# Retention in one fixed order of TensorE, the combine softmax taken once, and the zeros in longer rows

## The chip, the cores and the metric

The kernel runs on one core of a Trainium2 chip. The metric is the time of one launch on the device in microseconds (us), the median of three runs. A core has TensorE (PE, with its weight loads as PEld), VectorE (DVE), ScalarE (ACT), GpSimd (POOL) and SyncE (SP). Each works through its own list of instructions in order. SP issues most of the DMA transfers here, which 16 DMA engines carry out.

## The reference

Retention over q, k, v (4 batches, 8 heads, 768 tokens, 64 wide) gives x of 3072 tokens by 512. A soft mixture of experts with 32 slots follows, and after it a noisy top-2 mixture with 8 experts of width 1024.

```python
for t in range(S):                                   # retention
    state = gamma * state + einsum('bhd,bhe->bhde', k[:, :, t], v[:, :, t])
    y[:, :, t] = scale * einsum('bhd,bhde->bhe', q[:, :, t], state)
logits = x @ phi                                     # soft mixture, phi: 512 x 32
d = softmax(logits, axis=0)                          # dispatch: over the 3072 tokens
slot_out[e] = relu((d.T @ x)[e] @ w1[e]) @ w2[e]     # 8 experts, 4 slots each
c = softmax(logits, axis=1)                          # combine: over the 32 slots
x2 = c @ slot_out
noisy = x2 @ w_gate + log1p(exp(x2 @ w_noise)) * noise   # top-2 mixture
out[mask] += top2_w * (relu(x2[mask] @ v1[e]) @ v2[e])
```

## The kernel before

All arithmetic of the retention is f32. The kernel has four stages one after the other.

**Retention.** The 3072 tokens are 24 chunks of 128, six to a batch. `comp` holds q and the spread k and v of even chunk pairs, `raws` the k and v as they land. A chunk j needs, on TensorE: `k_t` (four transposes of k into `pt`, L273, copied to `kT` by ACT), `q_t` (the same for q, L262, scaled to `qT` by two products on DVE), `qk` (L283, eight matmuls into `pa`; two DVE products with the mask make `am`, L287), `y_out` (the part from the state, L301, four matmuls of `sbd` by `qT`, left out at the first chunk of a batch; then L305, eight matmuls of v by `am`; DVE scales `py` to `xT`, L308), `kv` (L316, the state in `pS`; ACT copies its two halves to `sbd`, L321) and `x_n` (L326, `xT` turned back, copied by ACT to `x`). ACT spreads k into each chunk's layout (two copies, L246), POOL spreads and scales v (L247).

Every four chunks `todo` brings five pieces of the soft mixture: `group0` (L336, the logits `pl`, copied to `LT`; the running maximum on DVE; the exponential `dT` on ACT), `group1` (L362, `dT` turned), `group2` (L371, the dispatch product `pp`, added to `acc` by DVE), `group3` (L380, `LT` turned; the combine softmax over the slots in `cs` by DVE and ACT; two DMAs to `ctab`, L393) and `group4` (L398, `cs` turned into `cT`). The loop on j writes these pieces down in one order, but the scheduler of the framework sets the order of each engine by its own estimate of times, save where `after` ties an instruction behind another. TensorE's list therefore has pieces of one product between those of another.

SP's list carries q, k and v (512 KB each for a pair of chunks), 28 pieces of 512 KB of the first weights W1 (L456), and 24 DMAs that write zeros to `out` (L460, 256 KB each, in rows of 512 bytes, from a tile `zt` of 128 by 128 that DVE makes anew for each, in two buffers, L459). A piece of W1 is paced by a one-element copy on DVE that reads `xT` (L455).

**Slots.** After the last chunk the last group's pieces, the sum over the tokens and `psi` (L507); then the loop `ph` over eight experts (L516, W1) with the last `group3` after e = 2 and the last `group4` after e = 3; then the loop `po` over eight experts (L549, W2), with a filler of six matmuls on ones (L142) ahead of e = 7, and W2 loaded by SP as buffers come free.

**Routing** (the logits of the second mixture, the top two, the lists of tokens) and the **main mixture** stand after that, and the change doesn't touch their code; they read `cT`, `ctab` and `out`.

What sets the order of the loads, and the pace of the loop, stands in these lines:

```python
if g == 0 and t and t + 1 < NT:
    load_kv(t + 1)             # the DMAs and the copies of a pair, one call
...
for i in range(NCH * (j - 1) // ZP, NCH * j // ZP if j <= ZP else 0):   # ZP = 21
```

Of the kernel before, what the change touches and what calls it, by code (L numbers as in the profile page):

```python
# [21 lines left out]
P = 128  # L22
# [17 lines left out]
ZP = 21  # L40
# [4 lines left out]
RL = 1  # L45
FS, FU, FV = 10, 2, 2
# [57 lines left out]
def kernel(ctx: ExitStack, tc: tile.TileContext, q, k, v, phi, w1, w2,  # L104
# [61 lines left out]
    cT = ab.tile([P, NG, P], F32, name="cT")  # L166
# [37 lines left out]
    with ExitStack() as actx:  # L204
# [22 lines left out]
        def load_kv(u, gs=range(2)):  # L227
            b, t = divmod(u, NC // 2)
            raw = RAW.setdefault(u, [])
            for i, src in enumerate(() if raw else (k, v)):  # L230
                x = raws[:, 2 * (u % 2) + i]
                nc.sync.dma_start(x.rearrange("p h r d -> p h (r d)"),
                                  src[b, :, 256 * t:256 * t + 256, :].rearrange("h (p r) d -> p h (r d)", r=2))
                raw.append(x)
            for g in gs:
                j = 2 * u + g
                if u % 2:
                    KL[j] = io.tile([P, H, D], F32, name="kl", bufs=2)
                    VL[j] = io.tile([P, H, D], F32, name="vl", bufs=2)
                else:  # L240
                    KL[j], VL[j] = (comp[:, 2 + i].rearrange("p h r d -> p (h r d)")[:, DM * g:DM * g + DM]
                                    .rearrange("p (h d) -> p h d", h=H) for i in range(2))
                gs = slice(64 * g, 64 * g + 64)
                for r in range(2):
                    rs = slice(64 * r, 64 * r + 64)
                    nc.scalar.copy(KL[j][rs], raw[0][gs, :, r, :])  # L246
                    pool_ins[0] = nc.gpsimd.tensor_tensor(VL[j][rs], raw[1][gs, :, r, :],  # L247
                                            gv[gs, r, t, :, None].to_broadcast([64, H, D]), op=OP.mult)
# [8 lines left out]
        def q_t(t, s):  # L257
            if s == 0:
                QT[t] = io.tile([P, HP, 2, P], F32, name="qT", bufs=2)
            pt = psA.tile([P, HP, P], F32, name="pt", tag="pt")  # L260
            for hp in range(HP):
                nc.tensor.transpose(pt[:, hp, :], QL[t][:, 2 * hp + s, :, :], ident)  # L262
            o = QT[t].rearrange("p h g (r i) -> p h g r i", r=2)
            i = pt.rearrange("p h (g i) -> p h g i", g=2)
            for r in range(2):
                rs = slice(64 * r, 64 * r + 64)
                nc.vector.tensor_tensor(o[64 * s:64 * s + 64, :, :, r, :], i[rs],  # L267
                                        gq[rs, :, s, None, :].to_broadcast([64, HP, 2, 64]), op=OP.mult)

        def k_t(j):  # L270
            pt = psA.tile([P, HP, P], F32, name="pt", tag="pt")
            for hp in range(HP):
                nc.tensor.transpose(pt[:, hp, :], KL[j][:, 2 * hp:2 * hp + 2, :], ident)  # L273
            KT[j] = io.tile([P, HP, P], F32, name="kT", bufs=2)
            return nc.scalar.copy(KT[j], pt)  # L275
# [18 lines left out]
        def y_out(j):  # L294
            t, g = divmod(j, 2)
            c = j % NC
            py = psA.tile([P, HP, P], F32, name="py")
            am = [AM.pop((j, s)) for s in range(2)]
            if c:
                for hp in range(HP):  # L300
                    nc.tensor.matmul(py[:, hp, :], sbd[c % 2][:, hp, :], QT[t][:, hp, g, :],  # L301
                                     start=(hp == 0), stop=False, skip_group_check=True)
            for hp in range(HP):
                for s in range(2):
                    nc.tensor.matmul(py[64 * s:64 * s + 64, hp, :], VL[j][:, 2 * hp + s, :],  # L305
                                     am[s][:, hp, :], start=(not c and hp == 0), stop=True, skip_group_check=True)
            XT[j] = work.tile([P, HP, P], F32, name="xT", bufs=4)
            nc.vector.tensor_tensor(XT[j], py, gy[:, c, :, None].to_broadcast([P, HP, P]), op=OP.mult)  # L308

        def kv(j):  # L310
# [3 lines left out]
            for hp in range(HP):  # L314
                for s in range(2):
                    nc.tensor.matmul(pS[64 * s:64 * s + 64, hp, :], KL[j][:, 2 * hp + s, :],  # L316
                                     VL[j][:, 2 * hp + s, :], start=(c == 0 and hp == 0),
                                     stop=True, skip_group_check=True)
            for s in range(2):
                r = slice(64 * s, 64 * s + 64)  # L320
                nc.scalar.copy(sbd[(c + 1) % 2][r, :, r], pS[r])  # L321

        def x_n(j):
            pt = psA.tile([P, HP, P], F32, name="pt", tag="pt")
            for hp in range(HP):
                nc.tensor.transpose(pt[:, hp, :], XT[j][:, hp, :], ident)  # L326
            X[j] = work.tile([P, DM], F32, name="x", bufs=5)
            nc.scalar.copy(X[j], pt.rearrange("p h e -> p (h e)"))

        GR, NM = {}, []  # L330

        def group0(g):
            pl = psA.tile([P, P], F32, name="pl", tag="pg", bufs=1)
            for kd in range(KD):
                for i in range(4):
                    nc.tensor.matmul(pl[32 * i:32 * i + 32, :], phis[:, kd, :], XT[4 * g + i][:, kd, :],  # L336
                                     start=(kd == 0), stop=(kd == KD - 1), skip_group_check=True)
            LT = small.tile([P, P], F32, name="LT", bufs=1)
            nc.scalar.copy(LT, pl)
            m = MZ[:, g:g + 1]  # L340
            z = MZ[:, NG + g:NG + g + 1]
            nc.vector.reduce_max(m, LT, axis=AX.X)
# [11 lines left out]
            nc.scalar.activation(dT, LT, AF.Exp, bias=nm, accum_out=z)  # L354
            if g:
                nc.vector.scalar_tensor_tensor(z, z0, al, z, op0=OP.mult, op1=OP.add)
            GR[g] = [LT, dT, al]

        def group1(g):
            LT, dT, al = GR[g]  # L360
            pd = psA.tile([P, P], F32, name="pd", tag="pg", bufs=1)
            nc.tensor.transpose(pd, dT, ident)  # L362
            dn = small.tile([P, P], F32, name="dn", bufs=1)
            nc.scalar.copy(dn, pd)
            GR[g] = [LT, dn, al]

        def group2(g):
            _, dn, al = GR[g]
            pp = psA.tile([P, DM], F32, name="pp", tag="pt")
            for i in range(4):  # L370
                nc.tensor.matmul(pp[32 * i:32 * i + 32, :], dn[:, 32 * i:32 * i + 32], X[4 * g + i],  # L371
                                 start=True, stop=True, skip_group_check=True)
# [4 lines left out]

        def group3(g):
            pl = psA.tile([P, P], F32, name="pln", tag="pg", bufs=1)
            nc.tensor.transpose(pl, GR.pop(g)[0], ident)  # L380
            cs = small.tile([P, 4, NS], F32, name="cs", bufs=1)
            nc.scalar.copy(cs, pl.rearrange("p (i s) -> p i s", s=NS))
            mx = small.tile([P, 4], F32, name="mx")
            nc.vector.reduce_max(mx, cs, axis=AX.X)
            nc.vector.tensor_tensor(cs, cs, mx[:, :, None].to_broadcast([P, 4, NS]), op=OP.subtract)
            nc.scalar.activation(cs, cs, AF.Exp)
            sm = small.tile([P, 4], F32, name="sm")
            nc.vector.reduce_sum(sm, cs, axis=AX.X)
            nc.vector.tensor_scalar_add(sm, sm, 1e-9)
            nc.vector.reciprocal(sm, sm)  # L390
            nc.vector.tensor_tensor(cs, cs, sm[:, :, None].to_broadcast([P, 4, NS]), op=OP.mult)
            for r in range(2):
                nc.gpsimd.dma_start(row_view(r)[:, 4 * g:4 * g + 4, :NS], cs[64 * r:64 * r + 64])  # L393
            GR[g] = cs

        def group4(g):
            pc = psA.tile([P, P], F32, name="pc", tag="pg", bufs=1)
            nc.tensor.transpose(pc, GR.pop(g).rearrange("p i s -> p (i s)"), ident)  # L398
            nc.vector.tensor_copy(cT[:, g, :], pc)

        NT = NCH // 2
        ov = out.rearrange("(p a) d -> p a d", p=P)
# [3 lines left out]
        load_kv(0, range(1))  # L406
        nc.scalar.dma_start(phis, phi.rearrange("(k p) s -> p k s", p=P))
        for s in range(2):
            q_t(0, s)
        fill(psA, "py", FU)  # L410
        k_t(0)
        fill(psA, "py", FV)
        load_kv(0, range(1, 2))
        load_q(1)
        load_kv(1, ())
        qk0 = qk(0)
        with after(qk0):
            q_t(1, 0)
        todo = []
        for j in range(NCH + 1):  # L420
            t, g = divmod(j, 2)
            if g == 0 and t and t + 1 < NT:
                load_kv(t + 1)
            if j < NCH:
                if j + 1 < NCH:
                    kt = k_t(j + 1)
                    if j < 1:
                        with after(kt):
                            load_kv(1)
                    if todo:  # L430
                        todo.pop(0)()
                    qk(j + 1)
                tn, s = (t + 1, 1) if g == 0 else (t + 2, 0)
                if tn < NT:
                    q_t(tn, s)
                if todo:
                    todo.pop(0)()
                y_out(j)
                if g == 0 and t + 2 < NT:
                    load_q(t + 2)  # L440
                with after(*([qk0] if j == 0 else [])):
                    kv(j)
            if j:
                if j == NCH:
                    group0(NG - 1)
                x_n(j - 1)
# [4 lines left out]
                for i in range(28 * (j - 1) // WP, 28 * j // WP if j <= WP else 0):  # L451
                    if i % 4 == 0:
                        W1[i // 4] = (ringp if i < 8 else ringa).tile([P, 4096], F32, name="w", tag="w")
                    s = slice(1024 * (i % 4), 1024 * (i % 4) + 1024)
                    nc.vector.tensor_copy(W1[i // 4][0:1, s][:, 0:1], XT[j - 1][0:1, 0, 0:1])  # L455
                    nc.sync.dma_start(W1[i // 4][:, s], w1[i // 4].rearrange("(p k) n -> p (k n)", p=P)[:, s])  # L456
                for i in range(NCH * (j - 1) // ZP, NCH * j // ZP if j <= ZP else 0):
                    zt = small.tile([P, P], I32, name="zt")
                    nc.vector.tensor_single_scalar(zt, XT[j - 1][:, 0, :].bitcast(I32), 0, op=OP.bitwise_and)  # L459
                    nc.sync.dma_start(ov[:, i, :].rearrange("p (a d) -> p a d", d=P),  # L460
# [588 lines left out]
```

## Time and profile before

| | us |
|---|---|
| median of three runs | 605.98 (605.3 to 606.72) |
| profiled execution | 606.45 |
| its span (first to last instruction) | 604.7 |
| retention, 17.5 to 161.5 | 144.0 |
| last group and slots, 161.5 to 205.7 | 44.2 |
| routing, 205.7 to 240 | 34.3 |
| main mixture, 240 to 604.7 | 364.7 |

The profile is of one execution. Its times count from the first instruction, and 1.75 us of the profiled time lie around the span. Over the span TensorE is busy for 559.4 us, DVE for 265.1, ACT for 242.2 and POOL for 228.0; the mean granted clock of TensorE is 0.96 of full speed. In the views a busy time counts the instructions of an engine, an idle time in brackets is what an instruction waited before it started, and the name behind the arrow is what released it. "issue" stands for no releaser that the profile shows.

### The profile page before, as it was taken

Reading aid. Unit: us, or ns where it says so; the run is one execution under the profiler, and the core shown is the slowest. Engines: PE = TensorE matmul, PEld = TensorE weight load, DVE = VectorE, ACT = ScalarE, POOL = GpSimd, SP = SyncE. Lnnn points to the kernel's source line nnn. Section 1 sums busy time; section 2 is a strip of 40 time slices with the busy share of each in tenths; the row PEclk is TensorE's granted clock in tenths of the full one; section 3 lists DMA queues with packets and bytes.
Section 4 is the critical chain, followed back from the end, with each engine's and each line's share of the span. In section 5 each row is a group of like instructions: output and inputs, shape, how many; then the busy total and the mean of one; then the engine's idle time right before and its main releaser. Section 6 shows DMA issues by size and latency. Waiting matters only on the chain.

```text
span 604.7 us, 10806 instructions
## 1 busy us (share of the span) xinstructions
PE 559.4 (93%) x4176; PEld 426.2 (70%) x4176; DVE 265.1 (44%) x581; ACT 242.2 (40%) x536; POOL 228.0 (38%) x223
## 2 busy tenths in 40 slices
PE   6999799999999888988999999999999999999991
PEld 3887677878744444676888788787787787788780
DVE  3766676776420065873432433324325235144200
ACT  2563455545300025334534445336236246254210
POOL 2543533342211045345453552543444445432231
PEclk8999899999989985989999999999999999999996
DMA  9999999897689953335556566567566544553332
GB/s 251 267 328 300 284 279 312 246 321 263 246 330 420 400 180 120 93 102 165 114 142 149 132 155 181 113 161 183 94 169 177 116 135 54 110 143 46 41 40 33
DMA packets 88062, 111.77 MB, mean 185 GB/s; under 512 B 10482, under 2 KB 64306, under 8 KB 86722
## 3 DMA queue, kind: packets, MB, share of 16 engines
q1 hardware_dynamic: 73840, 94.75, 49.0%
q0 software_dynamic: 9952, 14.37, 16.3%
q10 hardware_dynamic: 4210, 1.87, 1.2%
q8 instruction: 35, 0.57, 0.4%
q14 instruction: 25, 0.20, 0.1%
HBM read 87.92 MB, written 20.41 MB: 179 GB/s over the span
## 4 chain that ended last, share of the span: by engine, by line
PE 52%; DMA 3%; DVE 2%; issue 1%; POOL 0%; POOLq 0%; ACT 0%
PE pyc L873 13%; PE pyc L875 13%; PE pyc L874 13%; PE phc L840 4%; DMA out_dram<-yo,lsa 3%; PE pyc L879 2%; PE pyc L877 2%; PE pg L183 2%; DVE bta L744 1%; PE ptc L806 1%; DVE oh L736 1%; PE pli L747 1%; DVE bma L725 0%; POOL out_dram L854 0%; DVE hhl L845 0%
## 5 line engine op out<-in xcount | busy, mean ns | idle before, releaser
L873 PE MATMUL pyc<-wh,hhl 128*128 128x512 f32 x384 | 154.4, 402 | 0.0
L875 PE MATMUL pyc<-wh,hhl 128*128 128x512 f32 x384 | 152.4, 397 | 0.0
L874 PE MATMUL pyc<-wl,hhl 128*128 128x512 f32 x384 | 150.9, 393 | 0.0
L854 POOL DMA_INDIRECT out_dram<-yo,lsa x49 | 77.0, 1570 | 158.7 <-ACT w L891 42.9
L845 DVE SCALAR_TENSOR_TENSOR hhl<-phc,hhl 128x512 fp32r<-128x512 f32 (+1 forms) x128 | 66.7, 551 | 74.6 <-ACT hhl L843 70.5
L875 PEld LDWEIGHTS pyc<-wh,hhl 128*128 128x128 f32 x384 | 72.3, 188 | 16.9
L874 PEld LDWEIGHTS pyc<-wl,hhl 128*128 128x128 f32 x384 | 72.8, 189 | 15.3
L873 PEld LDWEIGHTS pyc<-wh,hhl 128*128 128x128 f32 x384 | 72.5, 189 | 14.9 <-issue 0.4
L882 ACT ACTIVATE yo<-pyc,cg 128x512 f32<-128x512 f32 x48 | 33.0, 688 | 115.6 <-PE pyc L875 93.2
L843 ACT ACTIVATE hhl<-phc 128x512 fp32r<-128x512 f32 (+1 forms) x128 | 59.0, 515 | 12.4 <-PE phc L840 10.4
L821 DVE TENSOR_TENSOR wl<-w,wh 128x1024 fp32r<-128x1024 f32 x32 | 39.1, 1225 | 56.0 <-ACT wh L815 55.9
L787 POOL DMA_INDIRECT cg<-ctab,lsa x49 | 50.1, 1023 | 20.7 <-issue 15.0
L815 ACT CAST wh<-w 128x1024 fp32r<-128x1024 f32 x32 | 33.5, 1049 | 34.5 <-DMA w<-in_moe_w_dram 26.6
L247 POOL TENSOR_TENSOR comp<-raws,cta 64x512 f32<-64x512 f32 x24 | 25.0, 1043 | 49.0 <-PE pS L316 13.6
L287 DVE TENSOR_TENSOR am<-pa,cta 128x512 f32<-128x512 f32 x48 | 32.5, 689 | 18.7 <-PE pa L283 15.7
L840 PE MATMUL phc<-cts,gs 128*128 128x256 f32 (+1 forms) x192 | 37.7, 307 | 2.7 <-DVE hhl L845 1.5
L840 PEld LDWEIGHTS phc<-cts,gs 128*128 128x128 f32 x192 | 30.2, 196 | 11.0 <-issue 2.5
L267 DVE TENSOR_TENSOR qT<-pt,cta 64x512 f32<-64x512 f32 x48 | 33.0, 688 | 10.1 <-PE py L301 4.7
L247 POOL TENSOR_TENSOR vl<-raws,cta 64x512 f32<-64x512 f32 x24 | 25.0, 1040 | 25.7 <-PE pS L316 13.1
L321 ACT COPY sbd<-pS 64x256 f32<-64x256 f32 x40 | 14.7, 367 | 48.3 <-PE pS L316 47.9
L283 PE MATMUL pa<-qT,kT 64*128 64x128 f32 x384 | 29.5, 296 | 1.8 <-ACT kT L275 1.8
L283 PEld LDWEIGHTS pa<-qT,kT 64*128 64x128 f32 x384 | 24.8, 198 | 8.7 <-ACT kT L275 6.6
(191 smaller groups left out, 733.3 us busy)
## 6 DMA issues: line engine op xcount, KB each, us to landing
w<-in_moe_w_dram SPq DMA_DIRECT2D x77, 512.0 KB
w<-in_moe_w_dram SPq DMA_DIRECT2D x11, 2048.0 KB
comp<-in_q_dram SPq DMA_DIRECT2D x12, 512.0 KB
raws<-in_k_dram SPq DMA_DIRECT2D x12, 512.0 KB
raws<-in_v_dram SPq DMA_DIRECT2D x12, 512.0 KB
out_dram<-zt SPq DMA_DIRECT2D x24, 256.0 KB
gs<-gr SPq DMA_DIRECT2D x112, 32.0 KB
w<-in_moe_w_dram SPq DMA_DIRECT2D x2, 1024.0 KB
```

The lines of the kernel that those rows point to most:

```text
L247: pool_ins[0] = nc.gpsimd.tensor_tensor(VL[j][rs], raw[1][gs, :, r, :], gv[gs, r, t, :, None].to_broadcast([64, H, D]), op=OP.mult)
L283: mm = nc.tensor.matmul(pa[s][:, hp, :], KT[j][r, hp, :], QT[t][r, hp, g, :], start=True, stop=True)
L787: nc.gpsimd.indirect_dma_start(out=cg[:rows(b), i, :], out_offset=None, in_=ctab, in_offset=index(e, b, rows(b)))
L815: ins = nc.scalar.copy(wh, V2[e][:, 1024 * i:1024 * i + 1024])
L821: nc.vector.tensor_tensor(wl, V2[e][:, 1024 * i:1024 * i + 1024], WH[e][i], op=OP.subtract)
L840: nc.tensor.matmul(ph[:, w * i:w * i + w], GS[e][:, kf + i], CT[e, g][:, :w], start=True, stop=True)
L843: relu.append(nc.scalar.activation(h[:, :, :w], pv, AF.Relu))
L845: last = nc.vector.scalar_tensor_tensor(h[:, :, w + t0:w + t0 + 2 * P], pv[:, :, :2 * P], 0.0, h[:, :, :2 * P], op0=OP.max, op1=OP.subtract)
L854: nc.gpsimd.indirect_dma_start(out=out, out_offset=index(e, b, n), in_=y, in_offset=None, bounds_check=N - 1, oob_is_err=False, compute_op ...
L873: nc.tensor.matmul(py, hhl[:, kf, ts], wh, start=(kf == 0), stop=False)
L874: nc.tensor.matmul(py, hhl[:, kf, ts], wl, start=False, stop=False)
L875: nc.tensor.matmul(py, hhl[:, kf, tl], wh, start=False, stop=(kf == KF - 1))
```

## The change

- Each piece of TensorE's work in the retention is written through `put`, which ties it behind the last matmul of the piece put before. Iteration j has `k_t(j+2)`, the state part of `y_out` (now `inter(j)`), `q_t`, `x_n(j-1)`, then `qk(j+1)`, then `kv(j)` and the rest of `y_out(j)`. `group1` stands ahead of `qk` in iterations 6, 10, 14, 18, 22, `group0` behind it in 4, 8, ..., 20, `group2` behind it where `group1` is ahead. The pieces with one shape of tile (128 by 128, then 64 rows, then 64 columns) follow one another.
- `load_kv` only issues the DMAs, three pairs ahead; the copies of k (ACT) and v (POOL) are in `spread(j + 3)`.
- `group3` and `group4` are gone from the retention and from `ph`. `LT` keeps the logits of all six groups. `combine` takes the softmax for all 24 chunks at once in the `po` loop ahead of e = 1 (tiles of 128 by 24 by 32, two `ctab` DMAs), `combine_t` turns it ahead of e = 4 into `cT`, which is `LT`'s memory.
- The zeros are six DMAs of 1 MB, in rows of 2 KB, in iterations 11 to 16, each behind that iteration's piece of W1; their source is the end of W1[6]'s buffer, set to zero once by POOL ahead of the loop. DVE makes no `zt`.
- `x` has six buffers for five.

The core of the diff (lines that only return a matmul, and the old bodies of moved code, are cut):

```diff
-ZP = 21
+Z0, ZN = 11, 6
+XB = 6
-        def load_kv(u, gs=range(2)):
+        def load_kv(u):
...
+        def spread(j):
+            u, g = divmod(j, 2)
...
+                nc.scalar.copy(KL[j][rs], RAW[u][0][gs, :, r, :])
+                pool_ins[0] = nc.gpsimd.tensor_tensor(VL[j][rs], RAW[u][1][gs, :, r, :],
+                                        gv[gs, r, t, :, None].to_broadcast([64, H, D]), op=OP.mult)
...
+        def inter(j):
...
+            for hp in range(HP if c else 0):
+                mm = nc.tensor.matmul(PY[j][:, hp, :], sbd[c % 2][:, hp, :], QT[t][:, hp, g, :],
+                                      start=(hp == 0), stop=False, skip_group_check=True)
...
+        def put(f, *a):
+            with after(*([last[0]] if last[0] else [])):
+                mm = f(*a)
+            if mm is not None:
+                last[0] = mm
...
+        W1[E - 2] = ringa.tile([P, 4096], F32, name="w", tag="w")
+        zt = W1[E - 2][:, 3584:]
+        nc.gpsimd.memset(zt, 0.0)
...
+                if j + 2 < NCH:
+                    put(k_t, j + 2)
+                put(inter, j)
...
+                    put(q_t, tn, s)
+                if g == 0 and t + 3 < NT:
+                    load_q(t + 3)
...
+                put(x_n, j - 1)
+            if j % 4 == 2 and j > 4:
+                put(group1, j // 4 - 1)
...
+                    put(qk, j + 1)
+                if j % 4 == 0 and j:
+                    put(group0, j // 4 - 1)
+                if j % 4 == 2 and j > 4:
+                    put(group2, j // 4 - 1)
+                put(kv, j)
+                put(y_out, j)
+                if j + 3 < NCH:
+                    spread(j + 3)
+                if g == 0 and t + 3 < NT:
+                    load_kv(t + 3)
...
-                    zt = small.tile([P, P], I32, name="zt")
-                    nc.vector.tensor_single_scalar(zt, XT[j - 1][:, 0, :].bitcast(I32), 0, op=OP.bitwise_and)
-                    nc.sync.dma_start(ov[:, i, :].rearrange("p (a d) -> p a d", d=P),
-                                      zt.bitcast(F32)[:, None, :].to_broadcast([P, HP, P]))
+                if Z0 <= j < Z0 + ZN:
+                    with after(w_dma):
+                        a = NCH // ZN * (j - Z0)
+                        nc.sync.dma_start(ov[:, a:a + NCH // ZN, :],
+                                          zt[:, None, :].to_broadcast([P, NCH // ZN, DM]))
...
+        def combine():
+            cb = [P, NCH, NS]
+            for i in range(2):
+                pl = psB.tile([P, G3, P], F32, name="pln", tag="pt")
+                for g in range(G3):
+                    nc.tensor.transpose(pl[:, g, :], LT[:, G3 * i + g, :], ident)
+                nc.scalar.copy(cs[:, 12 * i:12 * i + 12], pl.rearrange("p g (i s) -> p (g i) s", s=NS))
+            nc.vector.reduce_max(mx, cs, axis=AX.X)
+            nc.vector.tensor_tensor(cs, cs, mx[:, :, None].to_broadcast(cb), op=OP.subtract)
+            nc.scalar.activation(cs, cs, AF.Exp)
...
+            for r in range(2):
+                nc.gpsimd.dma_start(row_view(r)[:, :, :NS], cs[64 * r:64 * r + 64])
...
+            if e == 1:
+                combine()
+            if e == 4:
+                combine_t()
```

What this does to the order is seen at three places. The first is TensorE's list in the retention, in the two iterations around a `group1`. Before, `inter` (py from `sbd`), `y_out` (py from `am`), `pd` and `pln` stand between one another as the scheduler put them:

```order
L336 MATMUL pl<-xT,phis 32x128 x16
L283 MATMUL pa<-qT,kT 128x128 x8
L262 MATMUL pt<-ct,comp 128x128 x4
L362 MATMUL pd<-ct,dT 128x128
L301 MATMUL py<-qT,sbd_107 128x128 x4
L305 MATMUL py<-am,comp 64x128 x8
L326 MATMUL pt<-ct,xT 128x128 x4
L380 MATMUL pln<-ct,LT 128x128
L273 MATMUL pt<-ct,kl 128x128 x4
L305 MATMUL py<-am,vl 64x128
L371 MATMUL pp<-x,dn 32x512 x4
L283 MATMUL pa<-qT,kT 128x128 x8
```

Now, from one `k_t` on, an iteration without and one with a `group1`:

```order
L277 MATMUL pt<-ct,kl 128x128 x4
L306 MATMUL py<-qT,sbd_107 128x128 x4
L265 MATMUL pt<-ct,comp 128x128 x4
L339 MATMUL pt<-ct,xT 128x128 x4
L288 MATMUL pa<-qT,kT 128x128 x8
L328 MATMUL pS<-comp 64x64 x8
L316 MATMUL py<-am,comp 64x128 x8
L277 MATMUL pt<-ct,comp 128x128 x4
L306 MATMUL py<-qT,sbd_105 128x128 x4
L265 MATMUL pt<-ct,comp 128x128 x4
L339 MATMUL pt<-ct,xT 128x128 x4
L377 MATMUL pd<-ct,dT 128x128
```

`pd` now stands two iterations behind its `pl`, where it stood two pieces behind, and every product is whole.

The second place is ACT's list in the retention, around the spread of k into `comp` for an even chunk. Before, the copies (`comp<-raws`, with a wait on a DMA) follow a chunk's `kT`:

```order
L328 COPY x<-pt 128x512 [waits PE_49]
L275 COPY kT<-pt 128x512 [waits PE_49,Activation_49]
L246 COPY comp<-raws 64x512 [waits DMAHW7_49]
L246 COPY comp<-raws 64x512
L339 COPY LT<-pl 128x128 [waits PE_49]
```

Now they stand between the copy of `x` and the copies of the state (`sbd<-pS`):

```order
L279 COPY kT<-pt 128x512 [waits PE_49,Activation_49]
L341 COPY x<-pt 128x512 [waits PE_49]
L249 COPY comp<-raws 64x512 [waits DMAHW1_49,Activation_49]
L249 COPY comp<-raws 64x512 [waits Activation_49]
L333 COPY sbd_105<-pS 64x4x64 [waits PE_49]
```

Behind the copy that waits for the landing of k now stands the state that the next iteration's `inter` needs.

The third place is TensorE's list in the slots stage. Before, one turn of `cs` stands in `ph`, and `po` follows undivided:

```order
L516 MATMUL ph<-w,siT 32x256 x64
L398 MATMUL pc<-ct,cs 128x128
L516 MATMUL ph<-w,siT 32x256 x64
```

Now `pln`, the turn of the logits, stands in `po` (five of the six ahead of e = 0), and `pcn`, the turn of `cs`, behind the first matmul of e = 4:

```order
L532 MATMUL ph<-w,siT 32x256 x128
L561 MATMUL pln<-ct,LT 128x128 x5
L596 MATMUL po<-w,ht_2194 32x512 x8
L561 MATMUL pln<-ct,LT 128x128
L596 MATMUL po<-w,ht_2195 32x512 x8
L596 MATMUL po<-w,ht_2194 32x512 x8
L596 MATMUL po<-w,ht_2195 32x512 x8
L596 MATMUL po<-w,ht_2194 32x512
L578 MATMUL pcn<-ct,cs 128x128 x6
L596 MATMUL po<-w,ht_2194 32x512 x7
```

The whole softmax of 24 chunks has to be done between `pln` and `pcn`.

## Rows read from the trace of the kernel before

**Rows 1.** Windows by stage: length, busy us of each engine (instructions), granted clock, DMA.

```profile
17.50:161.50 144.00, 132.62 (x1697) 110.10 (x1696) 99.74 (x225) 73.26 (x161) 55.02 (x58) 0.99 0.95 285
...
189.00:205.70 16.70, 15.63 (x133) 4.26 (x133) 0.00 (x0) 0.00 (x0) 2.07 (x14) 1.00 1.03 419
205.70:240.00 34.30, 27.80 (x221) 16.23 (x222) 16.76 (x38) 12.33 (x24) 14.93 (x22) 0.74 0.56 192
240.00:604.70 364.70, 346.31 (x1736) 274.24 (x1735) 136.66 (x285) 147.39 (x334) 145.97 (x114) 0.98 0.52 119
```

**Rows 2.** Waits of TensorE's weight loads, 17.5 to 161.5: total us, times, longest.

```profile
PEld pd L362 <- ACT dT L354: 6.1, 5, 1.4
PEld pa L283 <- ACT kT L275: 5.2, 16, 0.8
PEld pt L273 <- issue: 3.1, 2, 3.0
```

**Rows 3.** Waits of DVE in the same stretch.

```profile
DVE zt L459 <- DMA out_dram<-zt: 6.8, 4, 3.2
```

**Rows 4.** Timeline, 59 to 67: start us, us, engine, line, operation, tiles, count [idle].

```profile
60.91 0.99 DVE L459 TENSOR_SCALAR zt<-xT 128x128 int32<-128x128 int32 x1 [3.17 <-DMA out_dram<-zt]
...
63.94 0.63 PE L273 MATMUL pt<-ct,comp 128*128 128x128 f32 x4 [2.74 <-DVE qT L267]
```

**Rows 5.** Timeline of the weight loads, 120 to 149.

```profile
122.84 0.81 PEld L336 LDWEIGHTS pl<-xT,phis 128*32 128x32 f32 x32 [0.17 <-issue]
123.88 0.97 PEld L283 LDWEIGHTS pa<-qT,kT 64*128 64x128 f32 x16 [0.23 <-ACT kT L275]
124.98 0.42 PEld L262 LDWEIGHTS pt<-ct,comp 128*128 128x128 f32 x4
126.82 0.14 PEld L362 LDWEIGHTS pd<-ct,dT 128*128 128x128 f32 x1 [1.42 <-ACT dT L354]
126.82 1.03 PEld L301 LDWEIGHTS py<-qT,sbd 128*128 128x128 f32 x8
127.97 0.85 PEld L305 LDWEIGHTS py<-am,comp 128*64 128x64 f32 x16
128.99 0.42 PEld L326 LDWEIGHTS pt<-ct,xT 128*128 128x128 f32 x4 [0.17 <-issue]
...
130.53 0.16 PEld L371 LDWEIGHTS pp<-x,dn 128*32 128x32 f32 x8 [0.17 <-ACT cs L382]
131.53 0.97 PEld L283 LDWEIGHTS pa<-qT,kT 64*128 64x128 f32 x16 [0.84 <-ACT kT L275]
...
139.61 0.60 PEld L316 LDWEIGHTS pS<-vl,kl 128*64 128x64 f32 x16
140.28 0.42 PEld L326 LDWEIGHTS pt<-ct,xT 128*128 128x128 f32 x4
140.66 0.47 PEld L273 LDWEIGHTS pt<-ct,comp 128*128 128x128 f32 x4
```

**Rows 6.** Instructions by line on DVE and ACT, 17.5 to 161.5: busy us, mean ns.

```profile
L287 DVE TENSOR_TENSOR am<-pa,cta 128x512 f32<-128x512 f32 x46 | 31.2, 689 | 13.9 <-PE pa L283 10.9 <-PE py L305 2.5
L267 DVE TENSOR_TENSOR qT<-pt,cta 64x512 f32<-64x512 f32 x42 | 28.9, 688 | 5.7 <-PE py L301 4.7 <-PE pt L262 0.3
L308 DVE TENSOR_TENSOR xT<-py,cta 128x512 f32<-128x512 f32 x23 | 15.7, 684 | 9.7 <-PE pl L336 9.7
...
L246 ACT COPY kl<-raws 64x512 f32<-64x512 f32 x23 | 14.2, 617 | 0.3
```

**Rows 7.** Windows in which q, k, v land (10 to 20), and W2 (200 to 210).

```profile
10.00:20.00 10.00, 8.72 (x78) 7.31 (x79) 3.82 (x6) 4.88 (x9) 8.05 (x8) 0.66 1.20 290
...
200.00:210.00 10.00, 7.57 (x77) 3.63 (x76) 0.52 (x2) 0.59 (x1) 0.00 (x0) 0.93 1.03 407
```

**Rows 8.** Timeline, 160 to 174: end of the retention, start of `ph`.

```profile
161.68 0.69 DVE L308 TENSOR_TENSOR xT<-py,cta 128x512 f32<-128x512 f32 x1 [2.02 <-PE py L305]
...
172.13 2.36 PE L516 MATMUL ph<-w,siT 128*32 128x256 f32 x20
```

**Rows 9.** Timeline of the weight loads, 186 to 210: the last expert of `po`.

```profile
204.55 0.16 PEld L549 LDWEIGHTS po<-w,ht 128*32 128x32 f32 x8 [1.81 <-DMA w<-in_moe_w_dram]
```

## What was predicted before the changed kernel ran

> **What bounds the kernel now.** I read the windows by stage first: they show the reader who is busy where the change is. In the retention TensorE is busy for 132.62 of 144.00 us at a clock of 0.99, DVE for 99.74, ACT for 73.26, and the DMA share is 0.95 at 285 GB/s [rows 1]. So TensorE is the first bound, with 11.4 us idle beside it, and the transfers are close behind. A busy TensorE isn't one at its peak: its busy time holds switches and small gaps, so the timeline has to give the price of each piece from start to start.
>
> The waits come next, and here one looks for what has nothing to do with arithmetic. TensorE's loads wait 6.1 us for `dT` ahead of `pd`, 5.2 us for `kT` ahead of `qk`, and 3.1 us ahead of `k_t` [rows 2]. The last is one stall of 2.74 us: DVE sat 3.17 us in the making of a zero tile, whose buffer an earlier write to `out` still held, and the products behind it, `qT` among them, came late [rows 4]. DVE lost 6.8 us to such writes in all [rows 3]. So about 14 us of TensorE's idle loads are waits that the order or the zeros make. The main mixture behind (364.7 us) and the routing only shift, since their code and data stay.
>
> **The retention, priced from the timeline** [rows 5]. Four transposes of `x_n` take 0.38 us to the next start (140.28 to 140.66), and 0.39 I take for `k_t` and `q_t` too, as equal pieces. `inter` and its change of shape take 1.15 (126.82 to 127.97), 1.04 without the change. The rest of `y_out` takes 1.02 (127.97 to 128.99). `qk` takes 1.10 (123.88 to 124.98), `kv` 0.67 with a change (139.61 to 140.28), 0.60 behind a piece of the same shape or nearly. `x_n` with the change to `qk` is 0.60.
>
> A whole iteration is then 0.39 + 1.04 + 0.39 + 0.60 + 1.10 + 0.60 + 1.02 = 5.14 us, and 24 are 123.4. Not there are four `inter` (4.2), four `kv` (2.4), two `k_t` and three `q_t` (2.0), one `x_n` and one `qk` (1.5), which are done ahead or don't exist: 113.3. A group costs `pl` 1.04 (122.84 to 123.88), `pp` 1.00 (130.53 to 131.53) and about 0.36 for `pd` and changes: 2.4, five of them 12.0. `group3` and `group4` would be there no more. From the stage's start at 17.5 that ends at 142.8 without any stall. Before, the last `xT` starts at 161.68 [rows 8], so a pipeline that never waits would gain 19 us.
>
> It will wait somewhere. I go through the engines by iteration. DVE has two `am`, two `qT` and one `xT`, 5 x 0.69 = 3.4 us of 5.14 [rows 6]: it fits, but the order binds. `x_n(j)` needs `xT(j)`, and that stands behind the second `am(j+1)`. `qk(j+1)` ends 1.62 us ahead of the end of `y_out(j)`, two `am` take 1.38, so `xT` starts on time, and `k_t`, `inter`, `q_t` (1.82 us) cover its 0.69. Where a batch starts there is no `inter`: the cover is 0.78, and with the waits between engines three times 0.75 are lost: 2.2 us. The last two iterations lack `q_t` and `k_t`: 1 us. In group iterations DVE has one product more (`acc`, 128 by 512 as the others) and `pp` waits for the copy of `x`: 0.4 each, 2 us. `pd` stands two iterations behind `pl` and waits no more; that wait goes whole.
>
> ACT has `kT`, `x`, two copies of k and two of the state, about 3.1 us of 5.14. In its list the copies of k stand ahead of the state's, and one of the first waits for a landing. If k is there they end before `kv` does. If it's late, `inter` is late by as much. Not covered at all I expect 1.5 us of that, from iterations 15 and 16. With the four terms the stalls are 6.7 us, of bounds 0 and 19 (below), and the retention ends at 149.5: about **12 us gained**. The value is nearer to the low bound since before's waits by name, 14 us, are of kinds that the order ends.
>
> **The transfers.** The stage moves 285 x 144 = 41.0 MB. Less time for the same bytes means 311 GB/s in 132 us. That was done: W2 alone reaches 407 to 419 [rows 1, 7]. The zeros are 6.3 MB. Rows of 512 bytes (q, k, v) move at 290 GB/s, longer ones at 407 [rows 7]: the zeros would take 15.5 us for 21.7. The trouble is their place. Iterations 11 to 16 hold all of them, nine pieces of W1 (4.7 MB, 11.6 us) and three pairs of q, k, v (4.7 MB, 16.3 us): 43.4 us of transfers in six iterations of 132/24 = 5.5, 33: 10 us too much. k and v are asked for three iterations before the spread needs them, 16 us, so the jam is mostly borrowed and paid back from iteration 17 on, where no zeros are. The bounds are 0 and 10 us; I took 1.5.
>
> The two rates stand in windows that differ in direction and source too [rows 7], so that the longer rows are no faster is among the rivals. The Trainium skill (DMA: Bandwidth & Descriptors, Specifications) has a rule on that side: from 512 bytes a transfer reaches line rate, so rows of 2 KB would bring nothing. The trace speaks against it, 290 GB/s against 407.
>
> **The tail and the slots.** From the last `xT` to `ph` are 10.45 us [rows 8]; the `group3` piece in it leaves: -0.5, of bounds 0 and -1. In `po` come six `pln` and six `pcn`, and a softmax that was spread over the retention. Its chain goes: two copies on ACT, maximum, difference, exponential, sum, quotient. Pieces of 768 elements, by 689 ns for 512 [rows 6], are 1.0 each on DVE (four) and 0.9 on ACT (617 ns for 512: one, and the copies together one); with the small ones about 6.3 us. An expert of `po` takes 1.7 (16.7 less the wait of 1.81 and a filler, through eight) [rows 1, 9], `pcn` stands behind four and starts 6.9 us after `po`; the chain starts after the first: about 1.0 us of wait, and twelve transposes cost 1.2. Yet the second half of e = 7 waits 1.81 us for its weights anyway [rows 9], and they don't wait for `po`; a delay of TensorE ahead of it is hidden up to there. What isn't hidden is the `ctab` writes, 3072 short rows that now share the engines with W2 at a DMA share of 1.03 [rows 1]. No row has them alone; bounds 0 and 2.5, I take +0.8, nearer to the side where the old pieces never showed.
>
> What else moves costs nothing that I see: POOL makes the zero tile ahead of the loop where it is idle, the sixth `x` only takes memory, and the copies on POOL have 55.02 us in 144 [rows 1]. W2's loads are bound to the buffers that the retention and `ph` free, so they shift along. Intervals at a lower granted clock, as in the routing (0.74) [rows 1], can fall otherwise after a shift: 3 us either way, for the range.
>
> **Sum.** 606.45 - 12 - 0.5 + 0.8 = 594.75 for the profiled execution; the median is 0.5 below that execution: **594 us**.
>
> **Rivals.**
> - *The jam isn't borrowed.* All 10 us of iterations 11 to 16 become waits of ACT for k in place of 1.5: 8.5 us more, about 602.5. For it: SP's list is in order, and k and v of the next pairs stand behind 1 MB of zeros each time. Against: the lead of 16 us.
> - *Longer rows are no faster.* The zeros take 21.7 us at 290 GB/s, 6.2 more; the jam of 16.6 us is over the lead, and with the old 1.5 some 5 to 6 are waited for: 600. For it: the 290 may be what reading q, k and v costs and not their rows. Against: the two rates. This is what the skill's rule would give.
> - *The transfers are the bound already, and the order makes it worse (the slower side).* The DMA share is 0.95 [rows 1]. If 285 GB/s is what this mix can do, the 41.0 MB take 144 us in any order. Then each of eleven landings holds ACT, and behind it the state, which in the old list stood free; at 1.1 us each the whole gain of 12 us is gone, and from there on it is slower. With 1.3 and the slots' 0.8 it is 609. Against it: the old stage had writes in 512 byte rows, and stretches in which a stall on DVE held the issue itself.
> - *Hardly any stall is left.* 2 us for 6.7: 589. For it: all four stalls are small and DVE has 1.7 us spare in an iteration. Against: fixed order leaves nothing to slip into a gap.
> - *The gain is given back behind the retention.* W2's loads can't go faster than 419 GB/s, so if the slots stage were bound by transfers that start at a fixed time, an earlier `ph` would wait. The wait of 1.81 [rows 9] says that it is close; but the loads start when buffers come free, which shifts too. Given back in part it would be 597; I count it with the forecast.
>
> **How the numbers follow.** The forecast, 590 to 599, has a chance of 0.61; hardly any stall (583 to 590) 0.12; the jam, in part or whole (599 to 604.8), 0.09; longer rows no faster (599 to 602) 0.04; transfers as the bound without more (604.8 to 607.2) 0.04; slower 0.10. A measurement of this kernel can't tell less than 0.2%, 1.2 us, from no change. So faster is 0.61 + 0.12 + 0.09 + 0.04 = 0.86, the same 0.04, slower 0.10. The range goes from 585 to 604: it leaves out 0.04 of the second case, below, and the last two, above, 0.18 together.
>
> **What would show it.** Right: the retention some 132 us long, iterations of 5.1 to 5.6 us, no wait of `pd` for `dT` and none of DVE for `out`, and TensorE's waits at the three batch starts. In iterations 11 to 17 ACT's copies of k waiting on a DMA would show the jam, in every pair the slower case. In the slots, `pcn` waits for DVE by a microsecond, and e = 7 for W2 by less than before or as much. Wrong would be a retention above 140 us, waits of `x_n` for `xT` in every iteration, or `ph` to the end taking over 3 us more than before.

## The result, and the profile after

The changed kernel takes 598.48 us (median of four runs, 597.71 to 599.01) against 605.73 on the same chip: a ratio of 0.988 (0.985 to 0.992), 7.25 us less. 594 was forecast, within 585 to 604. The profiled execution took 597.71 us, with a span of 595.9, 8.8 less than before. The window of the retention, against [rows 1]:

```profile
17.50:154.00 136.50, 128.33 (x1696) 106.94 (x1697) 86.27 (x166) 70.07 (x149) 48.46 (x48) 0.96 0.95 298
```

The next rows mark the borders: the last `xT`, the first matmul of `ph`, the turn of `so` behind `po`.

```profile
154.75 0.69 DVE L319 TENSOR_TENSOR xT<-py,cta 128x512 f32<-128x512 f32 x1 [2.03 <-PE py L316]
...
164.55 1.94 PE L532 MATMUL ph<-w,siT 128*32 128x256 f32 x16
```

```profile
200.76 1.94 PEld L605 LDWEIGHTS pst<-ct,so 128*128 128x128 f32 x8 [1.61 <-ACT so L601]
```

Before, `po` began and ended so:

```profile
189.03 0.16 PEld L549 LDWEIGHTS po<-w,ht 128*32 128x32 f32 x8 [1.07 <-POOL ht L545]
...
206.36 1.94 PEld L558 LDWEIGHTS pst<-ct,so 128*128 128x128 f32 x8 [1.66 <-ACT so L554]
```

The last `xT` comes 6.93 us earlier (161.68 to 154.75) [rows 8]. From there to `ph` are 9.80 us for 10.45: -0.65. `ph` is 0.13 shorter. From the start of `po` (181.32 now) to the turn of `so` are 19.44 us for 17.33: +2.11. From there to the end are 395.14 for 398.34: -3.20. These sum to -8.80. I don't put the last one down to the change: the 14 profiled executions of this study, of kernels with the same code there, had 395.1 to 399.1. The granted clock of the 35 us after that row was 0.73 before and is 0.90 here, but it doesn't explain the difference: the run e3 below has 0.90 too, and 399.1 us.

An undisturbed iteration of the retention, in the timeline of the weight loads:

```profile
27.56 0.42 PEld L277 LDWEIGHTS pt<-ct,comp 128*128 128x128 f32 x4 [0.17 <-ACT sbd L333]
27.95 0.97 PEld L306 LDWEIGHTS py<-qT,sbd 128*128 128x128 f32 x8
28.84 0.47 PEld L265 LDWEIGHTS pt<-ct,comp 128*128 128x128 f32 x4
29.49 0.42 PEld L339 LDWEIGHTS pt<-ct,xT 128*128 128x128 f32 x4 [0.18 <-ACT kT L279]
30.08 0.97 PEld L288 LDWEIGHTS pa<-qT,kT 64*128 64x128 f32 x16 [0.17 <-issue]
31.17 0.55 PEld L328 LDWEIGHTS pS<-vl,kl 128*64 128x64 f32 x16
31.63 0.86 PEld L316 LDWEIGHTS py<-am,vl 128*64 128x64 f32 x16
32.66 0.42 PEld L277 LDWEIGHTS pt<-ct,comp 128*128 128x128 f32 x4 [0.17 <-issue]
```

32.66 less 27.56 are 5.10 us: the price of 5.14 was right, and the waits of `pd` for `dT` [rows 2] and of DVE for `out` [rows 3, 4] are not in the list of waits any more. But iteration 16, counted from 0 as in the code, looks like this:

```profile
104.83 0.42 PEld L277 LDWEIGHTS pt<-ct,kl 128*128 128x128 f32 x4 [0.17 <-issue]
111.17 1.78 PEld L306 LDWEIGHTS py<-qT,sbd 128*128 128x128 f32 x8 [5.92 <-ACT sbd L333]
112.83 0.87 PEld L265 LDWEIGHTS pt<-ct,comp 128*128 128x128 f32 x4
113.68 0.87 PEld L339 LDWEIGHTS pt<-ct,xT 128*128 128x128 f32 x4
114.88 1.61 PEld L288 LDWEIGHTS pa<-qT,kT 64*128 64x128 f32 x16 [0.33 <-issue]
```

`inter` waits 5.92 us for the state, and the pieces behind it run in nearly twice their time. ACT's timeline says why: the copy of k ahead of the state's copy waits for a DMA.

```profile
102.36 0.59 ACT L341 COPY x<-pt 128x512 f32<-128x512 f32 x1 [0.75 <-PE pt L339]
109.13 1.24 ACT L249 COPY comp<-raws 64x512 f32<-64x512 f32 x2 [6.18 <-DMA raws<-in_k_dram]
110.38 0.74 ACT L333 COPY sbd<-pS 64x256 f32<-64x256 f32 x2
...
119.69 0.60 ACT L249 COPY comp<-raws 64x512 f32<-64x512 f32 x1
```

And SP's timeline shows what stood ahead of that k: two writes of 1 MB of zeros, two pieces of W1 between them, and q; it was issued at 97.33 and there at 109.1.

```profile
92.56 0.43 SPq L479 DMA_DIRECT2D out_dram<-w  x1
93.08 2.60 SPq L475 DMA_DIRECT2D w<-in_moe_w_dram  x2
95.73 0.78 SPq L479 DMA_DIRECT2D out_dram<-w  x1
96.61 0.64 SPq L217 DMA_DIRECT2D comp<-in_q_dram  x1
97.33 4.94 SPq L233 DMA_DIRECT2D raws<-in_k_dram  x1
```

The copy that waited also stands early in ACT's list. It is that of chunk 21, since chunk 20's goes into memory from which `kv(16)` still reads at 117.63; chunk 20's is the one at 119.69. The code writes chunk 21's copy in iteration 18, and `k_t(21)` reads it at 129.61, but the scheduler, which still orders ACT, put it where ACT arrives at 102.95, in iteration 15. So ACT held up the state for a k that landed 10 us before the first copy that had to have it.

```profile
117.63 0.55 PEld L328 LDWEIGHTS pS<-comp 128*64 128x64 f32 x16 [0.20 <-issue]
...
129.61 0.42 PEld L277 LDWEIGHTS pt<-ct,comp 128*128 128x128 f32 x4 [0.17 <-issue]
```

The windows over the stretch of the stall show the clock that was granted behind the wait, 0.72 in the mean (a part of it at 1.2 GHz, the lower of the two levels, the rest at 2.4), and the transfers at 343 to 384 GB/s, with 63% and 235 GB/s only from 137 on:

```profile
97.00:110.00 13.00, 8.49 (x118) 6.42 (x114) 6.43 (x12) 4.00 (x8) 4.15 (x4) 0.98 1.07 343
110.00:121.00 11.00, 9.82 (x112) 8.87 (x112) 4.52 (x10) 6.25 (x16) 1.56 (x2) 0.72 1.05 384
121.00:137.00 16.00, 15.50 (x193) 12.59 (x193) 11.50 (x23) 8.16 (x16) 6.58 (x7) 1.00 0.92 316
137.00:155.00 18.00, 17.69 (x255) 13.92 (x253) 8.91 (x18) 6.15 (x16) 0.31 (x2) 1.00 0.63 235
```

### The profile page after: what moved, and what is told of

Same layout as the page of the kernel before. It is cut to its first block, busy times and chain, and to the rows that moved or that the text cites. A ratio compares the mean times of both kernels' runs of the same rounds, so it can differ in the third digit from the quotient of the medians.

```text
span 595.9 us, 10652 instructions
## 1 busy us (share of the span) xinstructions
PE 552.0 (93%) x4176; PEld 420.0 (70%) x4176; DVE 254.6 (43%) x521; ACT 243.1 (41%) x529; POOL 222.7 (37%) x214
## 5 line engine op out<-in xcount | busy, mean ns | idle before, releaser
L929 ACT ACTIVATE yo<-pyc,cg 128x512 f32<-128x512 f32 x48 | 33.0, 688 | 117.0 <-PE pyc L922 109.1
L306 PE MATMUL py<-qT,sbd 128*128 128x128 f32 x160 | 22.5, 285 | 5.7 <-ACT sbd L333 5.7
```

## The experiments

Each is a ratio to the kernel before on its own chip, with its 95% interval; 0.01 is 6 us. The change itself was measured on the first chip alone, so a difference from its 0.988 is one of two such ratios.

**No zeros.** The six DMAs are cut, so `out` isn't cleared.

> The changed kernel without its six DMAs of zeros (the kernel leaves out that out is cleared). Theory A, the jam: iteration 15 loses 8 us because k lands late behind zeros and W1 in the queue (5.9 us of waiting and about 2 us at half clock behind it). Without the zeros no copy of k waits for a DMA, the retention ends near 146 in place of 154.5, and the time falls by 8 us from 598.5 to about 590.5. Theory B, the transfers are the bound in any case: q, k, v and W1 alone keep the queue full, the wait stays in iterations 11 to 17, and at most 2 us are won, 596 to 598.

0.977 (0.972 to 0.982). No copy of k from iteration 1 on waits for a DMA, and the last `xT` starts at 146.73 for 154.75, 8.0 us earlier. Theory A holds in its size, B falls.

**Zeros spread.**

```diff
-                if Z0 <= j < Z0 + ZN:
+                for i in range(NCH * (j - 1) // 18, NCH * j // 18 if j <= 18 else 0):
                     with after(w_dma):
+                        nc.sync.dma_start(ov[:, i, :], zt)
```

> The same zeros in the same 2 KB rows, but as 24 DMAs of 256 KB spread over iterations 1 to 18, each behind a piece of W1. Theory A: no six iterations ask for more than they can have, no copy of k waits over 1 us, the retention ends near 147, about 591. Theory B: the bytes are the same, so the waits only spread over the iterations and the time stays within 2 us of 598.5.

0.991 (0.987 to 0.995), no better than the change. Theory A failed here: the stall shrank, but another came:

```profile
73.44 0.42 PEld L277 LDWEIGHTS pt<-ct,comp 128*128 128x128 f32 x4 [1.08 <-ACT x L341]
...
110.67 0.42 PEld L277 LDWEIGHTS pt<-ct,kl 128*128 128x128 f32 x4 [3.68 <-ACT x L341]
```

Both are `k_t` behind an ACT that waited for k. So six crowded iterations aren't the cause alone: zeros among the loads delay some k here too. Both waits are again at copies that stand early in ACT's list, by the same test those of chunks 15 and 21, so the run doesn't show whether late landings alone would cost anything.

**Zeros late.** Two writes each in iterations 17, 18, 19, when the last q, k and v have been asked for.

```diff
-                if Z0 <= j < Z0 + ZN:
+                for i in range(2 if 17 <= j <= 19 else 0):
                     with after(w_dma):
-                        a = NCH // ZN * (j - Z0)
+                        a = NCH // ZN * (2 * (j - 17) + i)
...
+                if j == 20:
+                    with after(w_dma):
+                        s, dst, src = load_w1(27)
+                        nc.sync.dma_start(dst, src)
```

> The changed kernel with its six DMAs of zeros two to an iteration in iterations 17, 18 and 19, behind the last q, k and v, and the last piece of W1[6] (whose memory the zeros come from) loaded behind them. Theory A, the place of the zeros in front of k makes the jam: no copy of k waits over 1 us, the retention ends near 146.5 as without zeros, W2 bears the 15 us more of transfers in a stretch where the engines move only 250 to 270 GB/s, and the time is 590 to 592. Theory F, what the retention gains is given back by W1's last part and W2, which come later into a slots stage that the transfers bound: 595 to 598.5.

0.979 (0.976 to 0.983), 590.87 us. Chunk 21's copy stands early here too, but its k, asked for at 93.20, is there when ACT comes to it at 100.07:

```profile
93.20 0.38 SPq L233 DMA_DIRECT2D raws<-in_k_dram  x1
...
100.07 1.26 ACT L249 COPY comp<-raws 64x512 f32<-64x512 f32 x2
...
145.01 0.69 DVE L319 TENSOR_TENSOR xT<-py,cta 128x512 f32<-128x512 f32 x1 [2.03 <-PE py L316]
```

The last `xT` starts at 145.01, and the transfers fill the stretch that was slack:

```profile
121.00:137.00 16.00, 15.97 (x232) 13.64 (x231) 9.64 (x20) 8.00 (x19) 3.27 (x4) 1.00 1.06 415
137.00:155.00 18.00, 15.38 (x159) 10.18 (x162) 6.69 (x19) 3.86 (x12) 2.60 (x4) 0.92 0.96 384
```

415 and 384 GB/s for 316 and 235. From the start of `po` (172.18) to the turn of `so` (191.26) are 19.08 us, not more than the change's 19.44, so W2 gave nothing back. Theory A holds in the form that e1 and this run share: with this list of ACT, k must not queue behind zeros. No run moves that one copy alone, so what its early place adds isn't measured. Theory F falls.

**Zeros in short rows.**

```diff
-                        nc.sync.dma_start(ov[:, a:a + NCH // ZN, :],
-                                          zt[:, None, :].to_broadcast([P, NCH // ZN, DM]))
+                        nc.sync.dma_start(ov[:, a:a + NCH // ZN, :].rearrange("p a (b d) -> p (a b) d", d=P),
+                                          zt[:, None, :P].to_broadcast([P, 4 * NCH // ZN, P]))
```

> The same six DMAs of zeros at the same places, but written in rows of 512 bytes. Theory A with longer rows faster: the zeros take about 6 us more of transfer time within iterations 11 to 17, all of it behind a queue that is already too long, so the time rises by 4 to 7 us to 602 to 605. Theory C, rows from 512 bytes up move at one rate: no change, within 1 us of 598.5.

0.996 (0.993 to 0.999), 4 to 5 us above the change's 0.988. The stall is a microsecond longer:

```profile
113.16 1.78 PEld L306 LDWEIGHTS py<-qT,sbd 128*128 128x128 f32 x8 [6.92 <-ACT sbd L333]
```

So rows of 2 KB are faster here; C, and with it the Trainium skill's rule that 512 bytes are enough (DMA: Bandwidth & Descriptors, Specifications), doesn't hold for this kernel. Of the 4 to 5 us the trace places 2.3 up to the end of the retention; it has 2.8 more behind the slots, where these kernels scatter anyway, so 2.3 is what the rows are shown to cost.

**The state first on ACT.**

```diff
                 if j + 3 < NCH:
-                    spread(j + 3)
+                    with after(*([sb_ins[0]] if sb_ins[0] else [])):
+                        spread(j + 3)
```

> The zeros stay in iterations 11 to 16; only ACT's order changes: the two copies of k for chunk j+3 stand behind the two copies of the state of chunk j. Theory A1, the place in ACT's list turned a late landing into a stall of the state: k lands as late, but the iteration goes on meanwhile, and of 8 us lost about 5 come back, 593 to 594. Theory A2, k is needed at once anyway by the next k_t: the wait only moves from inter to k_t, under 1.5 us are won, 597 to 598.5.

1.018 (1.012 to 1.024), 18 us slower than the change. Neither theory saw it: `k_t(j+3)` is the next piece, and now it waits for its copies in nearly every iteration:

```profile
PEld pt L277 <- ACT kl L249: 18.0, 10, 2.2
PEld pt L277 <- ACT comp L249: 12.2, 8, 1.5
```

From 15 us on no copy of k waits for a DMA, though the zeros stand where they stood; but the iterations are longer too, so what a late k costs by its place on ACT can't be read from this run.

**Only the zeros.** The kernel before, its zeros as the change has them.

```diff
-                    zt = small.tile([P, P], I32, name="zt")
...
+                if Z0 <= j < Z0 + ZN:
+                    with after(w_dma):
...
```

> The kernel before with one part of the change alone: the zeros as six DMAs of 1 MB in 2 KB rows in iterations 11 to 16 from the end of W1[6]'s buffer, none made on DVE. Theory D, TensorE's new order carries the gain: DVE's 6.8 us of waits for out are gone with the 2.95 us stall of TensorE they made, the jam stays, and the time is 602 to 606. Theory E, the zeros carry it: 597 to 600.

1.004 (1.001 to 1.007). The waits of DVE for `out` are gone and one on k has come (ACT's waits):

```profile
ACT kl L246 <- DMA raws<-in_k_dram: 6.0, 2, 5.2
```

Theory D: none of the gain is the zeros', and in that place and the old order they cost as much as they save.

**The sequence in an iteration**, with late zeros in all three. First, `qk(j+1)` moved up behind `k_t(j+2)`:

> The kernel with late zeros, qk(j+1) moved up to stand right behind k_t(j+2): one more change of tile shape in each iteration, and the pieces of 128 by 128 no longer together. Theory I, the grouping by shape carries a good part of the gain: two more changes of 0.1 to 0.2 us in 23 iterations, 5 to 9 us slower than late zeros alone, a ratio of 0.988 to 0.994. Theory J, what counts is how far each piece stands from what it waits for: the state and xT get 1.1 us more of cover and the waits of x_n (6.2 us) shrink by as much as the changes cost; within 3 us of late zeros alone.

0.987 (0.982 to 0.992); on the same chip 9.4 us behind the run e10 (0.974, below), which has late zeros and the `ctab` writes moved. An iteration:

```profile
29.01 0.42 PEld L277 LDWEIGHTS pt<-ct,comp 128*128 128x128 f32 x4 [0.17 <-ACT sbd L333]
29.60 1.22 PEld L288 LDWEIGHTS pa<-qT,kT 64*128 64x128 f32 x16 [0.17 <-issue]
30.94 0.97 PEld L306 LDWEIGHTS py<-qT,sbd 128*128 128x128 f32 x8
...
34.40 0.42 PEld L277 LDWEIGHTS pt<-ct,comp 128*128 128x128 f32 x4 [0.17 <-issue]
```

It takes 5.39 us for 5.10. `k_t` to the next start is 0.59 for 0.39 and `qk` 1.34 for 1.09, two changes of shape for 0.45, and the wait of `x_n` (0.18) is gone: 0.3 in 21 iterations are 6 us. The last `xT` comes 9.8 us later than in e10 (155.01 for 145.17), and the other 3.9 are four waits of `pp` for `dn`, since no `qk` stands between `pd` and `pp`:

```profile
54.96 0.16 PEld L387 LDWEIGHTS pp<-x,dn 128*32 128x32 f32 x8 [0.97 <-ACT dn L379]
```

So I holds, but a part of the loss is of the kind J names.

Then the pieces tied in the sequence of the kernel before:

> The kernel with late zeros and ties, but the pieces of an iteration tied in the sequence in which the kernel before writes them down: k_t(j+1), qk(j+1), q_t, inter, y_out, kv, x_n(j-1), with group1 and group2 one behind the other. Theory J, the distance between a product and what it waits for carries the gain: qk stands right behind its k_t and waits for the copy to kT by 0.6 + 0.3 us, three more changes of shape cost 0.4, in 23 iterations some 25 to 35 us: 612 to 625. Theory M, any fixed order does, since what it ends are the scheduler's split pieces: 590 to 597.

1.017 (1.011 to 1.022). `qk` waits for the copy of its own `k_t` in nearly every iteration:

```profile
PEld pa L288 <- ACT kT L279: 25.8, 22, 1.6
PEld pp L387 <- ACT dn L379: 5.3, 5, 1.2
```

J holds, M falls: this fixed order is slower than before, though its copies are made three chunks ahead.

Last, the change's sequence without the ties (`put` only calls its function):

> The kernel with late zeros, the pieces written in the same sequence but not tied behind one another, so that the scheduler sets the order by its own estimate. Its TensorE list differs from the tied one in four places. Theory K, the sequence that is written down and the copies made ahead carry the gain and the ties add little: within 2 us of late zeros alone, ratio 0.976 to 0.983. Theory L, the four places cost as the old order did: over 4 us slower.

0.973 (0.968 to 0.977), as e10 with ties on the same chip (0.974). The scheduler, given this sequence and the copies three chunks ahead, makes nearly the same list. K holds. No run has the sequence without the copies ahead, so what each is worth alone stays open.

**The combine softmax.** The `ctab` writes behind the last copy of `h`:

> The changed kernel with the two writes of ctab behind the copies for e = 7 on POOL in place of e = 6. The po loop ends 2.1 us later against its start than before. Theory G, the writes share the transfer engines with W2[7]: without them ahead, e = 7 waits for its weights by 0 to 0.3 us in place of 1.1, and 0.8 to 1.1 us are won. Theory H, W2 is later for another reason (its bytes against the earlier ph): the wait stays at 1 us and nothing is won.

0.990 (0.987 to 0.994), not to be told from the change. The wait of e = 7 for its weights (1.12 us in the change) is gone, and `po` to the turn of `so` is 19.02 for 19.44: the mechanism of G, at half its size. With late zeros as well:

> Zeros late as in the run that placed them in iterations 17 to 19, and the ctab writes behind the copies for e = 7. Theory G: e = 7 of po no longer waits for its weights (0.77 us there), and the ratio to the kernel before falls from 0.979 to 0.976 to 0.979, 589 to 591. Rival H: no change against the late zeros alone.

0.974 (0.969 to 0.978), 589.5 us: the best of these versions with e12, but no run tells it from late zeros alone. Its `po` takes 19.02 us, that of late zeros 19.08.

The softmax back in the retention (the old `group3` and `group4`, put in the fixed order; to have room, `cs` shares the memory of `dn`):

> The changed kernel with the combine softmax back in the retention, for each group of four chunks, in the fixed order (the turn of the logits behind x_n in iterations 7, 11, ..., that of cs behind x_n in 8, 12, ...), and for the last group in ph. By my prices the retention pays at most 0.39 us for each of nine or ten turns on TensorE and some DVE and ACT time, 2 to 5 us, and po gets 2.1 back: 599 to 602. Rival: the turns and DVE's work vanish in waits that are there anyway, and the time is 596 to 598.

0.998 (0.995 to 1.000), 5 to 6 us behind the change. But I made a wait of my own: the last `dn` waits for the `ctab` write of the group before, whose memory it shares, the tail takes 4.3 us longer, and `ph` with its two turns 1.3.

```profile
163.97 0.20 PEld L387 LDWEIGHTS pp<-x,dn 128*32 128x32 f32 x8 [3.16 <-ACT dn L379]
...
187.73 0.16 PEld L593 LDWEIGHTS po<-w,ht 128*32 128x32 f32 x8 [1.07 <-POOL ht L589]
...
204.31 1.94 PEld L602 LDWEIGHTS pst<-ct,so 128*128 128x128 f32 x8 [1.61 <-ACT so L598]
```

`po` to `so` is 16.58 us here, 2.86 less than in the change, and the turns cost about 0.1 in an iteration. Whether taking the softmax once pays stays open.

## Why the prediction was right

**The price of an iteration** (5.14) was within 1%, and the reasons to expect the gain were the right ones: the waits of `pd` and `kT`, the split pieces and the stall on DVE [rows 2 to 5]. The sequence carries it, together with the copies made ahead (e10 and e12 against e11 and e13, and e5 for the zeros).

**The small stalls** were over-sized. Three at the batch starts, one of 1 us at the end, 0.4 in each group: 5.2 us were expected. With late zeros, from `k_t(2)` at 17.28 to the end of `y_out` at 144.72 are 127.4 us, 2.1 over the sum without waits. The batch starts do lose 0.65 each, but not by `xT`:

```profile
50.62 0.42 PEld L339 LDWEIGHTS pt<-ct,xT 128*128 128x128 f32 x4 [0.65 <-ACT kT L279]
```

`x_n` waits there for the copy of `kT`, which frees the `pt` buffer it needs.

**The jam** is the step that failed: "mostly borrowed", 1.5 us. Iterations 15 and 16 together took 8.2 us more than with late zeros (19.47 from the start of `qk(16)` to that of `qk(18)`, for 11.28), some 2 of it at a lower clock behind the stall. The place and the mechanism were foretold, and the excess of 10 us of transfers too. What was wrong is the lead of three iterations, 16 us. It was 5.6: k was asked for at 97.33, 2.6 us after its buffer was free (94.74), when the zeros and the pieces of W1 ahead of it on SP had been issued, and ACT came to the first copy from it at 102.95, since chunk 21's copy has the early place. k landed 11.7 us after it was asked for. Even with late zeros the lead is 6.9 us (93.20 to 100.07). The prediction took the place of the copy from the code; ACT's list has it elsewhere. That rival was given 0.09 and came nearly whole. That the forecast is only 4.5 us off is due in part to the over-sized small stalls, and in part to luck: up to the turn of `so` the sum had -11.7 us and the trace has -5.6, and 3.2 of the difference came back in code that the change doesn't touch.

**The start.** In the change's execution the first two iterations ran partly at the lower clock and took 1.7 us longer than with late zeros (7.29 + 5.81 for 6.32 + 5.10); no term had that. In the run with zeros spread it was 2.5.

**The slots** cost 2.1 us for 0.8. By the starts in `po`: the sixth `pln` 0.8, `pcn` 1.3, and the eight fillers in one row 0.6 more than five: 2.8 to e = 7, of which its wait for weights absorbed 0.7 (1.81 to 1.12), not all, as these came later too. `pcn` itself waited for no softmax: the 0.86 ahead of it is what any such change of shape takes (0.84 ahead of the fillers), though the last product on `cs` ended only 0.1 us before it.

```profile
189.58 0.64 PEld L578 LDWEIGHTS pcn<-ct,cs 128*128 128x128 f32 x6 [0.86 <-issue]
...
198.99 0.16 PEld L596 LDWEIGHTS po<-w,ht 128*32 128x32 f32 x8 [1.12 <-DMA w<-in_moe_w_dram]
```

**The tail**, -0.5, measured -0.65. **Transfers as the bound** fell: with late zeros the retention, 10 us shorter, moves 313 GB/s, where 285 would have been the limit. **Longer rows** help, by 2.3 us as far as the trace shows it.

## What to carry to other kernels

Price an iteration from start to start and then look at each engine's own list for a copy that waits on a transfer ahead of a copy that the next iteration needs. Read its place from that list and not from the code: a lead that is counted in written iterations can be gone where a scheduler still orders the engine. Writes that nobody reads soon belong behind the last load that somebody waits for; spread among the loads they didn't help here. In a pipeline by hand it is the distance between a product and what it waits for that paid, and an order without it lost to the scheduler.

## What was not expected of the hardware

A wait of TensorE of 5.9 us was followed by pieces at about half speed (granted clock 0.72 in 110 to 121, a mean that holds both levels, 1.2 and 2.4 GHz), so the stall cost some 2 us more than its length. And the same code behind the slots took 395.1 to 399.1 us, with granted clocks from 0.73 to 0.90 at its start; the two don't go together.
